# Issue order of stores, a skipped block and weight loads where an expert stage meets a feed-forward

## The chip, the cores and the metric

The kernel runs on one core of one Trainium2 chip. The metric is the device time of one execution in microseconds (us); the lower, the better. The core has a matrix engine (TensorE, PE in the profile, with its weight loads as PEld), a vector engine (VectorE, DVE), a scalar engine (ScalarE, ACT), GpSimd (POOL) and SyncE (SP), which here issues nearly all DMA transfers. Each engine works through its own instructions in the order of the program and waits on semaphores for the others. Transfers issued by SP stand in one queue.

## What is computed

Three layers in a row over 4608 tokens of width 512, all in float32: a decayed attention, a mixture of eight experts with one expert per token, and a feed-forward with squared ReLU.

```python
def _moe_ref(x, modality_id, w_gate, modality_bias, w1, w2):
    logits = x @ w_gate + modality_bias[modality_id]
    e_idx = np.argmax(logits, axis=1)
    ...
    for e in range(E):
        mask = e_idx == e
        h = np.maximum(x[mask] @ w1[e], 0.0)
        out[mask] = gate_w[mask, None] * (h @ w2[e])
    return out

def _moe2_ref(x, w_in, w_out):
    h = np.maximum(x @ w_in, 0.0)
    return h * h @ w_out
...
    x = attention output, (4608, 512)
    x = _moe_ref(x=x, **moe_kwargs)
    return _moe2_ref(x=x, **moe2_kwargs)
```

## The kernel before, in words

A float32 product is made of three products of halves: each operand is split into a high and a low part (names ending in h and l), and `three` and `six` issue the matmuls high x high, high x low, low x high (L787 to L789 in the expert stage, L1133 to L1135 in the feed-forward).

**The expert stage** (`phase12`) works on slots, groups of tokens of one expert. There are ten slots: "E" and 0 to 7 with 512 tokens each, and slot 8 (`NF`) with 256. Every slot has eight steps f = 0 to 7, so there are 80 steps, i = 0 to 79; step i = 71 is (`NF-1`, 7), and i = 72 to 79 are those of slot 8. In a step, `first` multiplies x by 128 columns of w1 and ScalarE and VectorE make hh and hl of the result (L803, L804), and `second` multiplies these by w2 into the banks y. TensorE is given `first` of step i+1 before `second` of step i. In slot 8 `first` and `second` are 12 matmuls each. The weights come as 80 blocks of 512 KB: `wload` (L400) loads one into a buffer wr, of which there are three, and `wsplit` splits it (L149 on ScalarE, L150 on VectorE) into a buffer wx (for w1) or wy (for w2) of the pool `wp`, which has ten. The function `wl` issues the loads up to three blocks ahead of the split. At f = 7 the finished slot is copied to ye and stored: yd<-ye (L834, "token sum" store, 1 MB, or 0.5 MB for slot 8) and sd<-ix (L835), which writes the token number of each place of the slot, 4 bytes each, to a table in device memory. GpSimd's later write of the next ix into the same buffer (L431) waits for that store.

**Work put among the last steps.** `combos` reads slot E's result back (eyr<-yd, L750), makes the seven products' operands x for the first feed-forward tile (t = 0) out of it, split into halves in the buffers x0 to x3, and stores each to xc (`put`, L762, 512 KB each) for later passes. `extras` writes out a block for tokens beyond the planned slots, which stands behind a branch (`tc.If`, L904); for these inputs it is skipped. It names its own buffers cwx, cwy, cwr and so on out of the same pools. On SP the far side of the skipped block has nine semaphore instructions, by which the engine takes up where its transfers stand, one for each lane of the queue and its own counter; the other engines wait there for their own counter alone. `wload2(m, j, pool)` loads weight block j of the feed-forward's matrix m (0 in, 1 out; w<-wc, L1012, two transfers of 896 KB each, halves); six calls make twelve transfers, into buffers of `cv` for (0, 0) and of `wp` for the others, which come free as the last steps finish.

**The feed-forward** (`phase3`) goes tile by tile, 9 tiles of 512 tokens in 3 passes. Its products are made with seven multiplications in place of eight. A unit of TensorE is `six` matmul groups issued as 6 matmuls per bank half; z (L1108, L1111) gathers the results and h (L1235, L1236) splits them for the second matrix. `Plan` takes all operations with model times and needs, and writes them out in the order of the model's start times; each engine then keeps that order. One stand-in operation of 8.0 us on the DMA queue opens the plan. `xprep(n)` prepares the next tile: it loads yr<-yd in two halves of 512 KB, copies and subtracts them into the buffers x (x<-yr, L1108 on ScalarE) and stores these to xc (L1124). A load of yr waits until the slots' yd have landed. Buffer x0 holds two operands, so a new x waits for the store of the old one to xc to be read out and for TensorE's last use.

Of the kernel before, what the change touches and what calls it, by code (L numbers as in the profile page):

```python
# [27 lines left out]
NF = 8  # L28
# [60 lines left out]
def kernel(ctx, tc, qT, kT, kN, vN, modT, w_gate, mbias, w1, w2, w_in, w_out,  # L89
# [574 lines left out]
    def phase12():  # L664
        with ExitStack() as c1:
# [79 lines left out]
            def combos():  # L745
                for _ in cs:
                    pass
                yr = cv.tile([P, KD, TS], F32, tag="w", name="eyr")
                tx = cv.tile([P, 2, 256], F32, tag="w", name="etx")
                sp.dma_start(yr, yd[:, 0:TS].rearrange("(c p) t -> p c t", p=P))  # L750
                yield 1
                xs = [cv.tile([P, 2, 2, 2, 256], F32R, tag="w", name=f"x{a}") for a in range(4)]
                b11, b12 = yr[:, 0:2, 0:256], yr[:, 0:2, 256:512]
                b21, b22 = yr[:, 2:4, 0:256], yr[:, 2:4, 256:512]

                def sub(o, a, b):
                    dve.tensor_tensor(out=o, in0=a, in1=b, op=ALU.subtract)

                def put(m, src):
                    t_ = held["x", m] = xs[m // 2][:, m % 2]  # L760
                    split(t_[:, 0], t_[:, 1], src, dve)
                    sp.dma_start(xc[0, m], t_.bitcast(F32).rearrange("p a k t -> p (a k t)"))  # L762

                sub(tx, b12, b11)
                put(0, b11)
                yield 1
                put(1, b21)
                yield 1
                sub(b12, b22, b12)
                put(2, b22)  # L770
                yield 1
                sub(b11, b22, tx)
                put(3, tx)
                yield 1
                put(5, b12)
                yield 1
                sub(b21, b21, b11)
                put(4, b11)
                yield 1
                put(6, b21)  # L780
                yield 1
# [28 lines left out]
            def second(u, cols=range(KD)):  # L810
# [9 lines left out]
                if f == 7:  # L820
# [5 lines left out]
                    if 3 not in cols:  # L826
                        return
                    ix = XG[s][1]
                    if s == "E":
                        yo, so = yd[:, 0:TS], sd[0:TS]  # L830
                    else:
# [6 lines left out]
            us = [(s, f) for s in seq for f in range(8)]  # L838
            wkeys = [(s, g) for s in seq for g in range(4)]
            nw = 2 * len(wkeys)  # L840
            st = {"ld": 4, "sp": 2}
            ex = combos()

            def wl(upto):
                while st["ld"] < min(upto, nw, st["sp"] + 3):
                    key = wkeys[st["ld"] // 2]
                    if key[0] not in ereg:
                        expert(key[0])
# [100 lines left out]
            for i, u in enumerate(us):  # L949
# [11 lines left out]
                    elif s != "E" and 3 <= f <= 6:  # L961
                        trans(nx, f - 3)
                if u == (NF, 7):
                    wload2(1, 0, wp)
                second(u)
                if s == "E" and f == 6:
                    trans(nx, 2)
# [18 lines left out]
                        pass  # L986
                    ws(8, 2, 11)
                else:
                    wl(i + 9)
                    fill(wsg(i + 6, 2 if i < 10 else 1, i + 9), part(cs, 2250))  # L990
                    if i >= 68:
                        run(ex, 3)
                    if i == 73:
                        assert next(cs, 0) == 0 and next(ex, 0) == 0
                        wload2(0, 0, cv)
                if u == (NF, 1):
                    wload2(0, 1, wp)
                if u == (NF, 4):
                    extras()
                if u == (NF, 5):  # L1000
                    wload2(0, 2, wp)
                if i == 6:
                    ext = nc.values_load(slots[0:1, 3, 0:1], min_val=0, max_val=NX)
            assert st["ld"] == st["sp"] == nw
# [77 lines left out]
    def phase3():  # L1082
        with ExitStack() as c2:
            ff = c2.enter_context(tc.tile_pool(name="ff", bufs=1))
            sb = lambda name, shape, dt=F32R: ff.tile(shape, dt, tag=name, name=name)
            plan = Plan()
            for j in (1, 2):
                wload2(1, j, wp, False)
            WT = [[[held["w", m, j, x] for x in range(2)] for j in range(3)] for m in range(2)]
            XT = [held["x", m] for m in range(7)]  # L1090
            HT = [sb(f"h{j}", [P, 2, 7, 256]) for j in range(3)]
# [204 lines left out]
            for n in range(9, len(T3)):  # L1296
                VO.append(VO[-1] if T3[n][1] == T3[n - 1][1] else 1 - VO[-1])
            plan.add([(DMA_, 8.0)], lambda e: None)
            loadw(0, 1, 1)
            for n, (p, t) in enumerate(T3):  # L1300
                nq = len(PASSES[p])
                order = sorted((7 * q + AT1[x], q, x) for q in range(nq) for x in AT1)
# [2 lines left out]
                if n + 1 < len(T3):  # L1305
                    if T3[n + 1][1] == t:
                        loadw(p + 1, 0)
                    xprep(n + 1)
                begin(n)
                for x in (1, 2, 5, 6, 7, 4, 3):  # L1310
# [45 lines left out]
```

## Time and profile before

| | us |
|---|---|
| median of 3 runs | 1433.48 |
| the runs | 1435.76, 1433.48, 1429.42 |
| profiled execution, as timed | 1429.32 |
| its span in the trace | 1427.6 |
| TensorE busy | 1359.1 (95% of the span) |
| VectorE, ScalarE, GpSimd busy | 1026.1, 632.1, 182.0 |
| feed-forward's first matmul | 657.7 into the span |

The three engines beside TensorE have room, so a change of the time shows where TensorE stands still or where its granted clock is low. The granted clock is given as a share of full speed: 1.00 is 2.4 GHz, 0.50 is 1.2 GHz. A wait is read together with what released it: an engine that waits for ScalarE may wait for a transfer that ScalarE waits for. In the rows "SPq" is SP's sequencer, "PEq" and "PEldq" that of TensorE.

### The profile page before, as it was taken

The page shows a single profiled execution, that of the slowest core. Times are in us where ns is not written, and L with a number is a line of the kernel's source. Part 1 is how long each engine was busy: PE and PEld are TensorE (multiplying, and loading weights), DVE is VectorE, ACT ScalarE, POOL GpSimd, SP SyncE. Part 2 cuts the span into 40 slices and gives each one's busy share as a digit, 9 for nine tenths or more (in the row PEclk, how much of TensorE's full clock was granted, in tenths as well). Part 3 has the DMA queues.
Part 4 walks back from the last instruction along what each step waited for, and adds up shares of the span by engine and source line. Part 5 has one row for each costly group of instructions (what it writes and reads, how often), then busy time and mean ns, then how long its engine had stood idle before and what let it go on. Part 6 is the DMA issues. An engine that isn't in the chain of part 4 may idle for free. (4 is left out here: it accounts for less than half of the span.)

```text
span 1427.6 us, 26428 instructions
## 1 busy us (share of the span) xinstructions
PE 1359.1 (95%) x10384; PEld 1250.9 (88%) x10384; DVE 1026.1 (72%) x2018; ACT 632.1 (44%) x1289; POOL 182.0 (13%) x164
## 2 busy tenths in 40 slices
PE   7999999999999999978899999999999999999994
PEld 6889877888788878868899999999999999999994
DVE  3777866877787788553788777777767777687674
ACT  1444444445445454342566555553334443343331
POOL 3222113101110010000212222100000000011122
PEclk9999999999999999998999999999999999999998
DMA  9977247988899897898544455587445564677672
GB/s 341 378 269 275 90 165 237 260 254 213 317 279 262 234 324 198 236 270 265 190 163 171 184 197 213 208 312 267 163 177 204 214 218 163 271 275 266 237 253 101
DMA packets 143733, 332.40 MB, mean 233 GB/s; under 512 B 20208, under 2 KB 54512, under 8 KB 143600
## 3 DMA queue, kind: packets, MB, share of 16 engines
q1 hardware_dynamic: 135520, 310.06, 65.0%
q0 software_dynamic: 5920, 19.40, 3.6%
q8 instruction: 83, 1.36, 0.4%
q10 hardware_dynamic: 2160, 1.17, 0.3%
q14 instruction: 50, 0.41, 0.1%
HBM read 222.57 MB, written 108.02 MB: 232 GB/s over the span
## 5 line engine op out<-in xcount | busy, mean ns | idle before, releaser
L1133 PE MATMUL bank<-w,h 128*128 128x256 f32 x1008 | 285.5, 283 | 16.1 <-ACT h L1235 5.8
L1134 PE MATMUL bank<-x,w 128*128 128x256 f32 x1008 | 285.9, 284 | 4.2 <-DVE x L1111 4.1
L1133 PE MATMUL bank<-x,w 128*128 128x256 f32 x1008 | 286.0, 284 | 2.3 <-DMA x<-xc 1.4
L1135 PE MATMUL bank<-w,h 128*128 128x256 f32 x1008 | 284.2, 282 | 1.2 <-DVE h L1236 1.1
L1135 PE MATMUL bank<-x,w 128*128 128x256 f32 x1008 | 285.3, 283 | 0.0
L1134 PE MATMUL bank<-w,h 128*128 128x256 f32 x1008 | 284.1, 282 | 0.0
L1108 ACT ACTIVATE z<-bank 128x256 f32<-128x256 f32 x288 | 110.4, 383 | 274.0 <-PE bank L1135 272.5
L1133 PEld LDWEIGHTS bank<-w,h 128*128 128x128 f32 x1008 | 191.6, 190 | 19.2 <-ACT h L1235 7.4
L1134 PEld LDWEIGHTS bank<-x,w 128*128 128x128 f32 x1008 | 193.5, 192 | 5.4 <-DVE x L1111 5.4
L1133 PEld LDWEIGHTS bank<-x,w 128*128 128x128 f32 x1008 | 193.1, 192 | 2.9 <-DMA x<-xc 1.6
L1135 PEld LDWEIGHTS bank<-x,w 128*128 128x128 f32 x1008 | 193.4, 192 | 0.0
L1135 PEld LDWEIGHTS bank<-w,h 128*128 128x128 f32 x1008 | 191.2, 190 | 2.2 <-DVE h L1236 2.2
L1235 ACT ACTIVATE h<-z 128x512 fp32r<-128x512 f32 (+2 forms) x270 | 156.9, 599 | 81.5 <-DVE z L1111 70.6
L1134 PEld LDWEIGHTS bank<-w,h 128*128 128x128 f32 x1008 | 191.3, 190 | 0.3 <-DMA w<-wc 0.2
L1236 DVE TENSOR_TENSOR h<-z,h 128x512 fp32r<-128x512 f32 (+2 forms) x270 | 173.3, 661 | 12.1 <-ACT h L1235 11.7
L1111 DVE TENSOR_TENSOR z<-z,bank 128x256 f32<-128x256 f32 x216 | 90.2, 418 | 63.1 <-PE bank L1135 42.3
L787 PE MATMUL bank<-hh,wy 128*128 128x512 f32 (+1 forms) x320 | 126.9, 397 | 5.7 <-ACT hh L803 5.7
L787 PE MATMUL bank<-xh,wx 128*128 128x512 f32 (+1 forms) x320 | 124.6, 389 | 3.9 <-PEq L904 3.9
L788 PE MATMUL bank<-xl,wx 128*128 128x512 f32 (+1 forms) x320 | 124.5, 389 | 1.1 <-DVE xl L743 1.1
L788 PE MATMUL bank<-hl,wy 128*128 128x512 f32 (+1 forms) x320 | 124.4, 389 | 1.0 <-DVE hl L804 1.0
L789 PE MATMUL bank<-xh,wx 128*128 128x512 f32 (+1 forms) x320 | 124.0, 388 | 0.0
L789 PE MATMUL bank<-hh,wy 128*128 128x512 f32 (+1 forms) x320 | 123.7, 387 | 0.0
(168 smaller groups left out, 2212.9 us busy)
## 6 DMA issues: line engine op xcount, KB each, us to landing
x<-xc SPq DMA_DIRECT2D x112, 512.0 KB
wr<-w SPq DMA_DIRECT2D x80, 512.0 KB
xc<-x SPq DMA_DIRECT2D x63, 512.0 KB
w<-wc SPq DMA_DIRECT2D x32, 896.0 KB
wc<-cwh SPq DMA_DIRECT2D x16, 896.0 KB
wc<-cwl SPq DMA_DIRECT2D x16, 896.0 KB
pd<-oe SPq DMA_DIRECT2D x24, 512.0 KB
xd<-xs SPq DMA_DIRECT2D x9, 1024.0 KB
```

The lines of the kernel that those rows point to most:

```text
L787: pe.matmul(ps, lh, rh, start=first, stop=False)
L788: pe.matmul(ps, lh, rl, start=False, stop=False)
L789: pe.matmul(ps, ll, rh, start=False, stop=last)
L1108: plan.add(a_(c), lambda e: e.activation(o, i, f), r, w)
L1111: plan.add(engs or d_(c), lambda e: e.tensor_tensor(out=o, in0=a, in1=b, op=op), r, w)
L1133: e.matmul(ps[n], lh, rh, start=first and n == 0, stop=False, skip_group_check=True)
L1134: e.matmul(ps[n], lh, rl, start=False, stop=False, skip_group_check=True)
L1135: e.matmul(ps[n], ll, rh, start=False, stop=True, skip_group_check=True)
L1235: plan.add(a_(c), lambda e: e.activation(h[:, 0, a:b], z[:, a + 1:b + 1], AF.Copy), rs, ks[0])
L1236: plan.add(d_(c), lambda e: e.tensor_tensor(out=h[:, 1, a:b], in0=z[:, a + 1:b + 1], in1=h[:, 0, a:b].bitcast(F32), op=ALU.subtract), rs + ...
```

## The change

Five things are done, all of them to the order in which work is issued.

1. The seven stores of the first tile's x to xc leave `combos` (L762). They are operations of the feed-forward's plan now, ahead of the preparation of the second tile.
2. `extras`, the skipped block, moves from the end of step (`NF`, 4) to the end of step (`NF-1`, 7), i = 71. All its lines count one higher in the changed file (L905 for L904).
3. At i = 70 and 71 the loads of expert weights go one block ahead of the split in place of three, and at i = 72 none is issued.
4. The feed-forward's weight loads are issued at other steps: (0, 1) at (`NF`, 2) for (`NF`, 1), (0, 2) at (`NF`, 4) for (`NF`, 5), (1, 0) at (`NF`, 5) for (`NF`, 7), (1, 1) at (`NF`, 7), and (1, 2) in the last `second`, ahead of the store of yd. The last two stood in the plan before.
5. The plan has no weight loads for its first pass any more; its stand-in of 8.0 us stays.

```diff
@@ combos / put
                     split(t_[:, 0], t_[:, 1], src, dve)
-                    sp.dma_start(xc[0, m], t_.bitcast(F32).rearrange("p a k t -> p (a k t)"))
@@ second
                     ix = XG[s][1]
+                    if s == NF:
+                        wload2(1, 2, wp)
@@ phase12
-            st = {"ld": 4, "sp": 2}
+            st = {"ld": 4, "sp": 2, "few": False}
...
-                while st["ld"] < min(upto, nw, st["sp"] + 3):
+                while st["ld"] < min(upto, nw, st["sp"] + (1 if st["few"] else 3)):
...
                 if u == (NF, 7):
-                    wload2(1, 0, wp)
+                    wload2(1, 1, wp)
                 second(u)
...
-                    wl(i + 9)
+                    st["few"] = i in (70, 71)
+                    if i != 72:
+                        wl(i + 9)
...
-                if u == (NF, 1):
+                if u == (NF, 2):
                     wload2(0, 1, wp)
+                if u == (NF - 1, 7):
+                    extras()
                 if u == (NF, 4):
-                    extras()
+                    wload2(0, 2, wp)
                 if u == (NF, 5):
-                    wload2(0, 2, wp)
+                    wload2(1, 0, wp)
@@ phase3
-            for j in (1, 2):
-                wload2(1, j, wp, False)
...
-            loadw(0, 1, 1)
...
+                    if n == 0:
+                        for m in range(7):
+                            dma(xc[0, m], XT[m].bitcast(F32).rearrange("p a k t -> p (a k t)"), 512,
+                                [("x", m, 0), ("x", m, 1)], [("xc", 0, m)])
                     xprep(n + 1)
```

What SP's queue holds shows the order. The first place is slot 7's stores and the skipped block, on SP before (wr are expert weights, w000 to w011 feed-forward weights):

```order
L834 DMA yd_93<-ye_5857 128x4x512
L835 REGISTER_ALU
L835 DMA sd_94<-ix_5146 128x4x1
L400 ISA
L400 DMA wr2_5876<-w2 128x2x512
L1012 DMA w000_5940<-wc_95 128x1792
L1012 DMA w001_5942<-wc_95 128x1792
L1012 DMA w010_5944<-wc_95 128x1792
L1012 DMA w011_5946<-wc_95 128x1792
L904 COMPARE_AND_BRANCH
```

The same place on SP after, up to the branch:

```order
L750 DMA eyr_5723<-yd_93 128x4x512
L400 ISA
L400 DMA wr2_5770<-w2 128x2x512
...
L835 DMA yd_93<-ye_5848 128x4x512
L836 REGISTER_ALU
L836 DMA sd_94<-ix_5146 128x4x1
L905 COMPARE_AND_BRANCH
```

And on SP after, from the far side of the skipped block to the first loads of yr:

```order
L400 DMA wr1_8934<-w1 128x4x256
L400 ISA
L400 DMA wr2_8936<-w2 128x2x512
L1017 DMA w000_8969<-wc_95 128x1792
...
L1017 DMA w121_9151<-wc_95 128x1792
...
L836 DMA sd_94<-ix_5525 128x2x1
L1127 DMA xc_97<-x0_5726 128x1024
L1127 DMA yr_9179<-yd_93 128x2x512
L1127 DMA xc_97<-x0_5726 128x1024
L1127 DMA yr_9179<-yd_93 128x2x512
```

Two loads of expert weights moved behind the block, the block directly behind sd of slot 7, and all twelve loads w000 to w121 ahead of the last yd and sd.

The second place is the start of the feed-forward on SP before, from the far side of the block:

```order
L1012 DMA w101_9124<-wc_95 128x1792
L832 TENSOR_LOAD slots_100
L832 ISA x2
L834 REGISTER_ALU
L834 DMA yd_93<-ye_9138 128x4x256
L835 REGISTER_ALU
L835 DMA sd_94<-ix_5525 128x2x1
L1124 DMA w110_9163<-wc_95 128x1792
...
L1124 DMA yr_9173<-yd_93 128x2x512 x2
```

There four weight loads stood between sd and yr; now two stores xc stand among the loads of yr, and the weights are ahead.

The third place is ScalarE in the first tile of the feed-forward, before (z gathers results, h splits them, x<-yr prepares the second tile):

```order
L1108 ACTIVATE z1_9171<-bank6_90 128x256
L1108 ACTIVATE z2_9172<-bank5_89 128x256
L1108 ACTIVATE z1_9171<-bank6_90 128x256
L1108 ACTIVATE z1_9171<-z1_9171 128x256
L1108 ACTIVATE z2_9172<-bank5_89 128x256
L1235 ACTIVATE h1_9168<-z1_9171 128x768
L1235 ACTIVATE h0_9167<-z0_9170 128x512
L1108 ACTIVATE z2_9172<-bank5_89 128x256
L1108 ACTIVATE x0_5726<-yr_9173 128x512
L1235 ACTIVATE h2_9169<-z2_9172 128x512
```

And ScalarE after, at the same place:

```order
L1111 ACTIVATE z1_9177<-bank6_90 128x256
L1111 ACTIVATE z2_9178<-bank5_89 128x256
L1111 ACTIVATE x0_5726<-yr_9179 128x512 x2
L1111 ACTIVATE z1_9177<-bank6_90 128x256
L1111 ACTIVATE z2_9178<-bank5_89 128x256
L1111 ACTIVATE z1_9177<-z1_9177 128x256
L1238 ACTIVATE h1_9174<-z1_9177 128x768
```

The two x<-yr copies moved up, from behind the third copy of z2 to directly behind the first, ahead of a copy of z1 and one of z2.

The matmuls of TensorE keep their order there up to the second half of the first tile (unit numbers count from 0; these are the first matmuls of units 14 to 18 after; each waits for the copy that frees its bank):

```order
L1136 MATMUL bank6_90<-x3_5729,w010_9004 128x256
...
L1136 MATMUL bank5_89<-x2_5728,w020_9064 128x256
...
L1136 MATMUL bank4_88<-x1_5727,w010_9004 128x256
...
L1136 MATMUL bank7_91<-x1_5727,w020_9064 128x256
...
L1136 MATMUL bank5_89<-x2_5728,w020_9064 128x256
```

Units 15 and 18 both write bank5, so the second waits until z2 of the first has been copied.

## Rows read from the trace of the kernel before

**Rows 1.** The page's busy times of each engine, over the whole span.

```profile
PE 1359.1 (95%) x10384; PEld 1250.9 (88%) x10384; DVE 1026.1 (72%) x2018; ACT 632.1 (44%) x1289; POOL 182.0 (13%) x164
```

**Rows 2.** Waits, 600 to 720 us, TensorE's: us in total, times, longest.

```profile
PE bank L1133 <- ACT h L1235: 5.8, 1, 5.8
PE bank L787 <- ACT hh L803: 5.7, 1, 5.7
PE bank L787 <- PEq L904: 3.9, 1, 3.9
```

**Rows 3.** Stretches: us, busy PE, PEld, DVE, ACT, POOL, PEclk, DMA share, GB/s.

```profile
634.40:640.10 5.70, 0.04 (x1) 0.04 (x1) 0.33 (x1) 1.42 (x3) 0.00 (x0) 0.69 0.93 208
640.10:644.00 3.90, 3.16 (x12) 2.67 (x12) 1.56 (x3) 0.18 (x1) 0.00 (x0) 0.50 1.02 418
...
648.00:653.00 5.00, 5.00 (x24) 5.00 (x24) 0.42 (x1) 0.39 (x1) 0.00 (x0) 0.50 0.64 234
...
657.70:676.80 19.10, 19.05 (x158) 18.67 (x156) 10.79 (x24) 7.51 (x18) 0.00 (x0) 1.00 0.94 226
661.00:670.00 9.00, 9.00 (x77) 9.00 (x76) 5.69 (x13) 4.90 (x13) 0.00 (x0) 1.00 0.91 51
670.00:681.00 11.00, 6.75 (x55) 6.37 (x53) 4.26 (x9) 1.42 (x3) 0.00 (x0) 1.00 0.95 388
676.80:682.60 5.80, 0.08 (x1) 0.09 (x1) 0.10 (x1) 1.28 (x3) 0.71 (x1) 0.86 0.65 255
```

**Rows 4.** Timeline of ScalarE, 608 to 683: start, us, what, [idle before, releaser].

```profile
610.18 1.15 ACT L149 ACTIVATE x<-eyr 128x512 fp32r<-128x512 f32 x2 [7.46 <-DMA eyr<-yd]
...
638.68 1.06 ACT L149 ACTIVATE wy<-wr 128x1024 fp32r<-128x1024 f32 x1 [9.55 <-DMA wr<-w]
...
667.23 0.39 ACT L1108 ACTIVATE z<-bank 128x256 f32<-128x256 f32 x1 [0.17 <-PE bank L1135]
...
681.32 0.63 ACT L1108 ACTIVATE x<-yr 128x512 fp32r<-128x512 f32 x1 [9.38 <-DMA yr<-yd]
```

**Rows 5.** Timeline of SP, 600 to 672: the transfers it issues.

```profile
604.42 0.51 SPq L750 DMA_DIRECT2D eyr<-yd  x1
...
624.49 0.39 SPq L835 DMA_DIRECT2D sd<-ix  x1
625.15 0.71 SPq L400 DMA_DIRECT2D wr<-w  x1
...
658.28 0.40 SPq L834 DMA_DIRECT2D yd<-ye  x1
...
659.56 2.98 SPq L1124 DMA_DIRECT2D w<-wc  x4
667.61 2.59 SPq L1124 DMA_DIRECT2D yr<-yd  x2
```

**Rows 6.** Timelines of SP and GpSimd: sd of two earlier slots.

```profile
483.13 0.39 SPq L835 DMA_DIRECT2D sd<-ix  x1
...
493.53 0.22 POOL L431 COPY ix<-tab 128x4 int32 x1 [27.15 <-DMA sd<-ix]
...
530.16 0.41 SPq L835 DMA_DIRECT2D sd<-ix  x1
...
544.24 0.29 POOL L431 COPY ix<-tab 128x2 int32 x1 [28.47 <-DMA sd<-ix]
```

**Rows 7.** Line L904, the skipped block: count, ns each, first and last start.

```profile
L904 SPq EVENT_SEMAPHORE  x9: 17/17/17, 639.3 to 648.5; - x9
L904 POOLq EVENT_SEMAPHORE  x6: 17/30/43, 558.1 to 560.1; - x6
L904 POOLq COMPARE_BRANCH  x1: 50/50/50, 555.8 to 555.8; - x1
...
L904 SPq COMPARE_BRANCH  x1: 53/53/53, 629.4 to 629.4; - x1
...
L904 PEldq COMPARE_BRANCH  x1: 6312/6312/6312, 641.5 to 641.5; - x1
```

## The prediction

> **What bounds the kernel now.** I first read the page's busy times: TensorE works 95% of the span [rows 1], so the time can change only where TensorE stands still or runs at the lower clock, and the stretch the edit touches is 600 to 700 us of the trace. The waits of that stretch name three stops of TensorE that belong together [rows 2]: 5.7 us for hidden values from ScalarE (L803), 3.9 us on its own sequencer at the skipped block (L904), 5.8 us for h from ScalarE (L1235) in the feed-forward. The stretch table puts them at 634.4 to 640.1, at about 644 to 648, and at 676.8 to 682.5, and shows the granted clock at 0.50 (the lower level, 1.2 GHz) after the first: 24 matmuls in 5.0 us, 0.208 each, against 158 in 19.05 us, 0.1206 each, at 1.00 [rows 3].
>
> Then I asked what stood behind each wait of ScalarE. Before 640 its split of the last weight block (wy) had waited 9.55 us for a load [rows 4] that SP issued at 625.15, directly behind the token-sum store yd and the index store sd (624.49) [rows 5]. Before 682.5 its copy x<-yr had waited 9.38 us [rows 4] for the loads of yr issued at 667.61; ahead of them in the queue lie yd, sd of the last slot (658.28 and the next issue) and four weight loads [rows 5]. In both places the queue is slow behind sd: from 661 to 670 it moves 51 GB/s, then 388 [rows 3]. This is no single event: sd of two earlier slots was issued at 483.13 and 530.16, and GpSimd's next write of ix, which waits for it, began at 493.53 and 544.24, 10.4 and 14.1 us later [rows 6]; the other slots lie between. A store of 2 KB therefore costs the queue as much as 4 MB of loads.
>
> **Stage A, up to the feed-forward.** The edit takes seven stores xc (0.5 MB each) out of SP's queue before yd/sd, and puts the skipped block directly behind sd of slot 7. What the skipped block does on SP: it leads past nine semaphore instructions [rows 7], which in the changed order wait for the last transfer of each lane of the queue; the lanes of yd and sd are among them. So SP leaves the block when sd has landed: 624.49 + 10.4 to 14.1 = 634.9 to 638.6, and I take the middle, 636.7. The weight loads of steps 78 and 79, one of which before was issued at 625.15 and the other earlier still, now follow the block. Issue costs 0.7 (624.49 to 625.15 [rows 5]). Landing: eyr, 1 MB, was used 5.76 us after its issue (604.42, 610.18 [rows 4, 5]); the half-size load less 0.5 MB at about 0.4 MB/us, 4.5, and 5.8 as upper end. 636.7 + 0.7 + 4.5 = 641.9 for ScalarE's split, 1.06 [rows 4], then hh at about 0.4 and a hand-over: TensorE, which by ScalarE's order has run dry after step 76's first half (about 633), goes on at R = 643.5 to 643.8, bounds 641.7 to 646.5. Eight halves of 12 matmuls are left, 96: about 25 at the lower clock as before (25 x 0.21 = 5.3), 71 at 0.1175 (8.35, an estimate from the 0.1206 above less idle records). The stage ends at 657.3 (655.3 to 660.2) against 657.7 before. The stop at L803 of 5.7 and the one at the block of 3.9 vanish, and one stop of 10 to 11 us takes their place: **net 0, -2 to +2.5.**
>
> The block itself moves on every engine. On TensorE it now comes while 512-wide matmuls run. The row of GpSimd, whose branch came amid ordinary traffic, lasts about 2.3 us (555.8 to the first semaphore at 558.1), TensorE's 6.3 at 641.5, amid the weight loads [rows 7]. The sequencer runs ahead by the 12 matmuls that were still executed after it branched (640.1 to 644 [rows 3]), some 2.5 us. So 2.3 is hidden, 6.3 leaves 3.8; I take 0.5, and any of it is swallowed by the wait until R, since TensorE stops there anyway.
>
> TensorE's branch at the block lasts 6312 ns [rows 7] and costs it 3.9 us [rows 2]. The Trainium skill, page "Advanced Engine Details and Errata", section "Control Flow Timing", gives about 108 ns for a compare-and-branch, with which this trace does not agree. By that figure alone the block would be passed in 0.1 us on each engine, SP would issue the next load at about 625.3, TensorE would resume near 640 and the sum below would be about +8 instead of +9.6, inside the forecast's own range.
>
> **Stage B, the start of the feed-forward.** All twelve weight loads (0.917 MB each) now stand in the queue ahead of yd and sd of the last slot, where before four stood behind them. With the two expert loads that is 12.06 MB from 637.4 on. At 0.41 MB/us (between 0.388 and 0.418 [rows 3]) this takes 29.4 us, with 1.5 for the start and for buffers that come free late: 668.3. TensorE needs yd's landing next: 0.5 MB, 1.3, 669.6. Then the slow 9 us behind sd, 678.6. Then xc0, yr#1, xc1, yr#2, 2.1 MB at 0.39, 5.4, and 0.6 as before between the end of such a sum and the use (670 + 4.2 MB/0.39 = 680.7, used at 681.32 [rows 3, 4]): 684.6, against 681.32 for the first half of yr before.
>
> What decides is where those copies stand on ScalarE. Before, x<-yr followed the z2 copy that frees TensorE's bank for unit 21, and TensorE went on to unit 26 (158 matmuls recorded in that stretch, 26 units of 6 [rows 3]). Now both x<-yr copies stand ahead of the z1 and z2 copies that follow the unit-12 copy of z2; unit 18 waits for the z2 copy of unit 15. TensorE stops after 18 units, at 657.3 + 18 x 0.72 = 670.3, until both copies (0.63 each [rows 4]; the second from 684.6) and two copies of 0.4 are through: 686.3. Before it resumed at 682.5 after 26 units. The lag is (686.3 - 682.5) + 8 units x 0.72 = 3.8 + 5.8 = **9.6 us**. The lower clock after the stop is as before. Low end: sd early (-1.8) and the slow time half as long (-4.5), since nothing shows how much of it belongs to the store and how much to what is queued: +3.3. High end: sd late (+1.9), landing 5.8 (+1.3), rate 0.388 (+1.7): +14.5.
>
> What follows is bound by TensorE, so the lag stays. The seven xc stores now run beside the second tile: 3.7 MB in a tile's time of over 20 us, behind yr, so at nothing; were the queue full there, the copies for the next tile would come up to 9 us late, against a whole tile of lead. Fewer DMAs at 611 to 622 give nothing: TensorE does not wait there [rows 2].
>
> **The sum.** 1429.3 (the profiled execution, as timed) + 0 + 9.6 = 1438.9. That execution is 4.2 us under the median of the three, 1433.5; against the median the sum is 1443.1.
>
> **Rivals.**
> Same: the slow time behind the last sd is short, because the queue is less deep behind it (four weight loads fewer). For it: that slot has 256 tokens, so its store is half as large. Against: 51 GB/s for 9 us was seen behind that very store [rows 3]. Result +3.3, 1432.6 here, 1436.8 against the median, within 0.5%, 7.2 us, which is about what a measurement can tell from no change.
>
> Faster: the nine waits are already met when SP comes, so the expert loads leave at 625 and the slow time is not the store's but came from the traffic around it (the seven xc writes before, now gone). Then the stops of 5.7 and 3.9 and the excess of 38 slow matmuls (38 x 0.09 = 3.4) go, 13 us, the stage ends near 645. That alone gains little: with a slow 9 us left, the second yr would be used at about 673 and TensorE resume at 675, lag -7.5 + 5.8 = -1.7. It decides only if the slow time behind the last sd is under some 3 us as well; then -11, 1418, 1422 against the median. Against it: the two sd rows of slots without any xc store [rows 6].
>
> Worse: SP's code for the far side of the block is fetched through the same slow queue. For it: SP's branch at 629.4 saw its first semaphore only at 639.3, 9.9 us later, and the last at 648.5 [rows 7]. If a second fetch falls after sd has landed, 4 us are added to R and to everything behind it: +13.6 to +15, 1447 to 1449 against the median. It counts as slower.
>
> **Chances.** The forecast (slower by 7 to 13) 0.45, worse 0.13, together 0.58 for slower by over 0.5%; same 0.30; faster by over 0.5% 0.12. The likeliest is the forecast: 1443. The forecast's own range is 1440 to 1447. The range to hold 8 in 10 takes in the same case down to -3.5, 1430, and the worse one to +17.5, 1451; below lie about 0.12, above 0.07.
>
> **What would show it.** In the changed kernel: SP's semaphore rows at L905 ending 10 to 14 us after sd of slot 7, at 635 to 639; one stop of TensorE of 9 to 12 us from about 633 for hh from ScalarE, and none at L905; the stage's end at 655 to 660; ScalarE waiting for yr from about 668 to 684, 15 us; a stop of TensorE of about 16 us after 18 units; 8 to 9 us at under 80 GB/s behind the last sd. Wrong would be: a wx load that lands before 635, a slow time under 4 us, or TensorE passing unit 18 before yr has landed.

## The result and the profile of the changed kernel

The changed kernel takes 1443.76 us (median of 6 runs, 1442.66 to 1449.85), the kernel before 1434.13 (6 runs, 1429.42 to 1436.9). The ratio is 1.0069 with a 95% interval of 1.0048 to 1.009: slower by 0.7%, 9.6 us between the medians. Forecast were a slower kernel, a lag of 9.6 us, and 1443 (1443.1 by its sum).

The profiled execution of the changed kernel took 1449.85, its slowest run, and that of before 1429.32, its fastest. So the traces are compared by stretches. The issue of sd of slot 7 stands at 624.49 before [rows 5] and at 631.87 after; these 7.4 us arose in the first 250 us, where the edit touches nothing (the first yd is issued at 248.52 and at 256.52).

| stretch | before, us | after, us | difference |
|---|---|---|---|
| up to the issue of sd of slot 7 | 624.49 | 631.87 | +7.4 |
| from there to the first matmul of the feed-forward (657.67, 664.44) | 33.18 | 32.57 | -0.6 |
| from there to the third pass, a wait of 0.47 us of TensorE for z at 1225.01 and 1242.76 | 567.34 | 578.32 | +11.0 |
| from there to the end of the span | 202.6 | 205.3 | +2.8 |

The last row is not the edit's either: TensorE's stops after 1200 us add up to 10.8 us before and 13.5 after, and to between 10 and 16 us in the traces of the experiments, in no order with the edits. By these two traces the edit did -0.6 + 11.0 = 10.4 us, beside the 9.6 of the medians and the 9.6 of the forecast.

The page of the changed kernel, busy times, answers to [rows 1]:

```profile
PE 1361.6 (94%) x10384; PEld 1254.7 (87%) x10384; DVE 1024.2 (71%) x2018; ACT 632.2 (44%) x1289; POOL 180.5 (12%) x164
```

TensorE has the same work in a longer span; the time went into its stops.

The waits of the changed kernel from 600 to 720 us answer to [rows 2] (us in total, times, longest):

```profile
PE bank L1136 <- ACT z L1111: 18.7, 1, 18.7
PE bank L786 <- DVEq L905: 7.6, 1, 7.6
...
PE bank L787 <- DVE hl L803: 0.9, 1, 0.9
PE bank L786 <- ACT hh L802: 0.8, 1, 0.8
```

The three stops of before have become two. One of 18.7 us at z in the feed-forward has replaced that of 5.8 at h, and one of 7.6 behind VectorE's sequencer at the block (DVEq L905) has replaced those of 5.7 and 3.9.

The stretch table of the changed kernel, with the columns of [rows 3], shows where TensorE stands and what the queue moves meanwhile:

```profile
629.90:637.50 7.60, 0.04 (x1) 0.00 (x0) 1.38 (x2) 2.25 (x4) 0.00 (x0) 0.81 0.47 144
649.50:664.40 14.90, 13.21 (x96) 13.02 (x97) 4.40 (x7) 4.00 (x10) 0.00 (x0) 0.89 0.99 399
664.40:677.50 13.10, 13.10 (x110) 12.94 (x108) 7.13 (x17) 4.84 (x12) 0.00 (x0) 1.00 1.01 414
677.50:696.20 18.70, 0.04 (x1) 0.00 (x0) 0.67 (x2) 1.79 (x5) 2.37 (x2) 0.63 0.71 177
...
680.00:690.00 10.00, 0.00 (x0) 0.00 (x0) 0.00 (x0) 0.00 (x0) 0.00 (x0) 0.62 0.39 36
```

In the third row TensorE runs 13.1 us into the feed-forward, which is 18 units of 0.72 (110 matmul records), and in the fourth it stands still. The last row is the slow time behind the last sd, 36 GB/s, with no engine at work.

The timeline of SP in the changed kernel, 631 to 690, answers to [rows 5] (start, length, what is issued):

```profile
631.23 0.40 SPq L835 DMA_DIRECT2D yd<-ye  x1
631.87 2.12 SPq L836 DMA_DIRECT2D sd<-ix  x1
645.36 1.17 SPq L400 DMA_DIRECT2D wr<-w  x2
646.59 18.37 SPq L1017 DMA_DIRECT2D w<-wc  x12
665.78 0.40 SPq L835 DMA_DIRECT2D yd<-ye  x1
...
688.21 0.39 SPq L1127 DMA_DIRECT2D yr<-yd  x1
...
689.17 0.42 SPq L1127 DMA_DIRECT2D yr<-yd  x1
```

And that of ScalarE, to [rows 4]:

```profile
648.87 1.06 ACT L149 ACTIVATE wx<-wr 128x1024 fp32r<-128x1024 f32 x1 [4.58 <-DMA wr<-w]
...
692.46 0.63 ACT L1111 ACTIVATE x<-yr 128x512 fp32r<-128x512 f32 x1 [18.08 <-DMA yr<-yd]
695.04 0.63 ACT L1111 ACTIVATE x<-yr 128x512 fp32r<-128x512 f32 x1 [1.95 <-DMA yr<-yd]
```

The last yd was issued at 665.78, behind twelve weight loads; yr could be issued only when it had landed, at 688.21, and was used at 692.46 and 695.04. SP's own waits in that stretch name the landing of yd:

```profile
SPq L1127 <- DMA yd<-ye: 15.1, 1, 15.1
```

TensorE went on at 696.26, 31.8 us into the feed-forward; before it went on at 682.52, 24.9 us into it, and had eight units more behind it.

The lines at the block in the changed kernel answer to [rows 7]:

```profile
L905 SPq EVENT_SEMAPHORE  x9: 17/17/17, 641.4 to 644.3; - x9
...
L905 PEldq EVENT_SEMAPHORE  x1: 51/51/51, 630.5 to 630.5; - x1
L905 DVEq COMPARE_BRANCH  x1: 72/72/72, 632.2 to 632.2; - x1
...
L905 DVEq EVENT_SEMAPHORE  x1: 21/21/21, 637.5 to 637.5; - x1
```

SP leaves the block at 644.3, 12.4 us after it issued sd. TensorE's own sequencer is past the block at 630.5, 0.6 us after the end of its last matmul at 629.9. VectorE comes to its branch at 632.2 and is past it at 637.5, and in the same instant, 637.55, TensorE goes on. So 2.3 of the 7.6 us of TensorE's stop lie before VectorE's branch (its split of wx, ahead of the branch, had waited 2.13 us for ScalarE's), and 5.3 between the branch and the far side.

### The profile page after: what moved, and what is told of

It reads as the page before. It is cut to its first block, busy times and chain, and to the rows that moved or that the text cites. A ratio compares the mean times of both kernels' runs of the same rounds, so it can differ in the third digit from the quotient of the medians.

```text
span 1448.1 us, 26435 instructions
## 1 busy us (share of the span) xinstructions
PE 1361.6 (94%) x10384; PEld 1254.7 (87%) x10384; DVE 1024.2 (71%) x2018; ACT 632.2 (44%) x1289; POOL 180.5 (12%) x164
## 5 line engine op out<-in xcount | busy, mean ns | idle before, releaser
L1136 PE MATMUL bank<-w,h 128*128 128x256 f32 x1008 | 285.1, 283 | 13.1 <-DVE oe L1114 7.8
L1239 DVE TENSOR_TENSOR h<-z,h 128x512 fp32r<-128x512 f32 (+2 forms) x270 | 172.0, 658 | 22.9 <-ACT h L1238 22.4
```

The lines of the kernel that those rows point to most:

```text
L1136: e.matmul(ps[n], lh, rh, start=first and n == 0, stop=False, skip_group_check=True)
L1239: plan.add(d_(c), lambda e: e.tensor_tensor(out=h[:, 1, a:b], in0=z[:, a + 1:b + 1], in1=h[:, 0, a:b].bitcast(F32), op=ALU.subtract), rs + ...
```

## The experiments

Three things were to be told apart: what part of the loss is the place of the copies on ScalarE, what part the order on the queue, and what the skipped block and the store sd cost by themselves. Each run's ratio is to the kernel before, run beside it on the same chip; since the median of before lay between 1435 and 1439 there, the ratios are compared, not the microseconds. The stretch "A" goes from the issue of slot 7's yd to the first matmul of the feed-forward, "B" from there to a wait of 0.69 us of TensorE for oe in the second tile, which every trace has (722.37 before, 740.08 after). Each kernel has one trace. Up to the feed-forward the changed kernel, e1 and e2 have the same order but for e2's last four weight loads, and their A is 33.2, 36.3 and 35.1: a difference of 3 us in A is no more than that spread.

| kernel | ratio (95% interval) | A, us | B, us |
|---|---|---|---|
| before | 1 | 33.8 | 64.7 |
| changed | 1.0069 (1.0048 to 1.0090) | 33.2 | 75.6 |
| e1 changed, copies late | 0.9932 (0.9910 to 0.9955) | 36.3 | 56.4 |
| e2 changed, two weight blocks behind | 1.0048 (1.0024 to 1.0073) | 35.1 | 72.5 |
| e3 before, stores xc late | 0.9980 (0.9960 to 1.0000) | 32.8 | 67.1 |
| e4 before, block early | 0.9993 (0.9974 to 1.0012) | 32.7 | 66.5 |
| e5 changed, sd on the other queue | 0.9989 (0.9973 to 1.0005) | 30.0 | 66.0 |
| e6 before, copies late | 0.9984 (0.9965 to 1.0004) | 34.8 | 62.3 |
| e7 before, both | 0.9926 (0.9898 to 0.9953) | 27.6 | 57.7 |
| e8 changed, both | 0.9945 (0.9923 to 0.9967) | 29.8 | 57.3 |
| e9 as e7, block in mid-slot | 0.9920 (0.9893 to 0.9947) | 21.4 | 57.6 |
| e10 as e7, block at a slot's end | 0.9969 (0.9947 to 0.9991) | 21.2 | 58.1 |
| e11 changed, no block | 1.0019 (1.0004 to 1.0035) | 30.2 | 72.9 |
| e12 before, no block | 0.9977 (0.9961 to 0.9994) | 27.5 | 66.1 |

In e9 and e10 the block's price lies ahead of A, since the block stands in an earlier slot.

### e1: the copies later on ScalarE

```diff
-            plan.add([(DMA_, 8.0)], lambda e: None)
+            first_ready = [("b", i, j) for i in range(2) for j in range(2)]
+            first_ready += [("xc", 0, m) for m in range(7)]
+            plan.add([(DMA_, 22.0)], lambda e: None, (), first_ready)
```

The stand-in operation had no operation depending on it, and the plan put it behind the loads of yr, whatever its length: with 16, 20, 24 or 28 us in its place the order of the first tile came out the same. Here the loads of yr and the stores xc depend on it.

> The changed kernel with one edit: the plan is told that xc and yr start 22 us into the feed-forward, so that ScalarE's two x<-yr copies stand some 20 rows later; the order on the queue up to the first four loads of yr and their neighbours stays. Theory (the loss is the place of the copies on ScalarE, in front of work that TensorE waits for): TensorE passes unit 18 without a stop, the 18.7 us stop becomes one of under 3 us, and the time falls by 14 to 18 us, to 1426 to 1430. Rival (the loss is the lateness of yr itself, whatever the order, because the second tile needs it): a stop of 10 us or more stands elsewhere and the time stays at 1440 or above.

Measured: 0.9932, which against the changed kernel's 1.0069 is 1.4%, 19 to 20 us; the two traces differ in B by 19.2 us, while A, with nothing changed in it, came out 3.1 longer. Waits of e1, 600 to 720 us:

```profile
PE bank L786 <- DVEq L905: 7.4, 1, 7.4
...
PE bank L786 <- ACT hh L802: 3.4, 1, 3.4
...
ACT x L1111 <- DMA yr<-yd: 2.9, 2, 1.5
PE bank L1136 <- ACT oe L1111: 1.4, 2, 0.7
```

The stop of 18.7 us is gone, and nothing took its place: yr came hardly earlier (issued at 690.01 and 690.97, 22 and 23 us into the feed-forward, in the changed kernel 24 and 25), but ScalarE waits for it 2.9 us in all and TensorE not at all. The rival falls. So the whole of the loss, and more, hangs on the order of the first tile's operations. The edit moved more than the two copies, though: the plan also put TensorE's first matmuls of the second tile, which in the changed kernel stand after 210 matmul records of the feed-forward, behind all 252 of the first tile. In the old order, without the stop, TensorE would have come to them about 27 us in (an estimate: 46.4 in the changed kernel's trace less the 19.5 by which the stop shifted them), and e1's two copies began 26.3 and 28.9 us in. With the copies alone moved, a wait of a few us for x may have been left; no run shows it. The gain is larger than expected because the stop of 5.8 us that the kernel before has in B is gone too.

### e2: two weight blocks behind the last yd and sd again

```diff
-                    if s == NF:
-                        wload2(1, 2, wp)
...
+                second(u)
                 if u == (NF, 7):
                     wload2(1, 1, wp)
-                second(u)
+                    wload2(1, 2, wp)
```

> The changed kernel with the feed-forward's weight blocks (1, 1) and (1, 2), 3.7 MB, behind the last yd and sd again, as before the change. Theory (yd has to queue behind the backlog of weights): yd lands about 8 us earlier after its issue, but yr then queues behind these 3.7 MB; x<-yr begins 2 to 5 us earlier than in the changed kernel, and the time is 1439 to 1442. Rival (the backlog does not matter, only the slow time behind sd): no difference, 1443 to 1445.

Measured: 1.0048; the intervals of e2 and of the changed kernel overlap, so the difference of 3 us between the ratios is inside what the runs can tell. In the traces B is 3.1 us shorter and A 1.9 longer. Waits of e2:

```profile
PE bank L1135 <- ACT z L1110: 15.7, 1, 15.7
PE bank L786 <- DVEq L903: 11.8, 1, 11.8
```

yr was issued 13.7 us after the last yd in place of 22.4, as expected, but its first use came 25.0 us into the feed-forward in place of 28.0, and 1.9 of these 3.0 us are the feed-forward's own later start: the stop at the block happened to be 4 us longer. That leaves 1.1 us for the backlog ahead of yd, if it is a part of the loss at all: what the queue does not carry ahead of yd, it carries ahead of yr.

### e3 and e4: one part of the change alone, in the kernel before

```diff
@@ e3: the stores xc go into the plan
-                    sp.dma_start(xc[0, m], t_.bitcast(F32).rearrange("p a k t -> p (a k t)"))
...
+                    if n == 0:
+                        for m in range(7):
+                            dma(xc[0, m], XT[m].bitcast(F32).rearrange("p a k t -> p (a k t)"), 512,
+                                [("x", m, 0), ("x", m, 1)], [("xc", 0, m)])
@@ e4: the block goes to the end of step 71
-                if u == (NF, 4):
+                if u == (NF - 1, 7):
                     extras()
```

e4 also holds the loads of expert weights back as the change does.

> The kernel before with one part of the change: the seven stores xc of the first tile go into the plan. The plan then puts x<-yr about five copies later on ScalarE than before, and the stores no longer stand ahead of yd and sd of slot 7. Theory: the expert stage keeps its stops of 5.7 and 3.9 (the load behind sd stays where it was, so the stores ahead did not make it slow), the stop of 5.8 at h goes since the copies stand later, and yr comes about 2.5 us later: 1426 to 1431. Rival (the seven stores ahead of sd made the queue slow): the stop of 5.7 at hh shrinks under 2.

> The kernel before with one part of the change: the skipped block moved to the end of step 71, with the loads of expert weights held back as in the change; the stores xc and the feed-forward's other loads stay as before. Theory: the stops of 5.7 and 3.9 go and one stop of 9 to 12 us for the weight load behind the block takes their place, so the start of the feed-forward moves by under 2.5 us and the time is within 1432 to 1437. Rival (the move of the block is the loss, not the start of the feed-forward): 1440 or above.

Measured: 0.9980 and 0.9993, intervals up to 1.0000 and 1.0012. Neither part is the loss by itself. Waits of e3, then of e4:

```profile
PE bank L786 <- PEq L903: 4.3, 1, 4.3
PE bank L786 <- ACT hh L802: 3.4, 1, 3.4
...
PE bank L1133 <- DMA w<-wc: 2.3, 1, 2.3
PE bank L1132 <- DMA w<-wc: 1.9, 1, 1.9
```

```profile
PE bank L787 <- DVEq L904: 10.3, 1, 10.3
PE bank L1135 <- ACT h L1237: 5.7, 1, 5.7
```

In e3 the stop at h is gone because the plan put x<-yr later, and two short stops for weight loads that stand behind sd came up instead: 2.9 us gained between the medians' ratios where 3 to 8 were expected, and in the trace A and B together are 1.4 us longer than before, so this stretch does not show the gain. The stop for hh fell from 5.7 to 3.4, between the two theories. In e4 the stops of 5.7 and 3.9 became one of 10.3, and A stayed within 1.2 us. The size was forecast, the name was not: it is VectorE's passage past the block and not the weight load that TensorE waits for.

### e5: the index store on GpSimd's queue

```diff
-                    sp.dma_start(so.rearrange("(j p) -> p j", p=P), ix[:, :wd // P])
+                    pool.dma_start(so.rearrange("(j p) -> p j", p=P), ix[:, :wd // P])
```

GpSimd also reads the slot's place into a register of its own.

> The changed kernel with one edit: the index stores sd of all slots are issued by GpSimd, on its own queue, instead of SP. Theory (the slow time is the store of 4-byte elements itself, and it holds up only the queue that it is in): SP leaves the skipped block some 3 to 5 us after yd's issue instead of 13, the weight loads behind the block come before ScalarE wants them, TensorE's stop at the block remains only as far as VectorE's code fetch takes (2 to 4 us); yr is issued 8 us sooner behind yd and the stop at unit 18 falls from 18.7 to 8 to 11. Together 10 to 16 us under the changed kernel, a ratio to the kernel before of 0.995 to 1.000. Rival (the small elements occupy the 16 DMA engines, whatever queue they come from): stops and ratio as in the changed kernel, 1.005 to 1.009.

Measured: 0.9989, 0.8% under the changed kernel. Waits of e5, then the issues of SP at the start of the feed-forward:

```profile
PE bank L1137 <- ACT z L1112: 8.4, 1, 8.4
PE bank L786 <- DVEq L906: 7.2, 1, 7.2
```

```profile
663.88 0.39 SPq L836 DMA_DIRECT2D yd<-ye  x1
...
675.46 0.39 SPq L1128 DMA_DIRECT2D yr<-yd  x1
```

yr goes out 11.6 us after the last yd, not 22.4. But GpSimd does not wait for yd: it issued the last two index stores at 566.61 and 578.50, long before SP's yd of slots 7 and 8 (632.14 and 663.88). Its store at 578.50, SP's next two transfers, and the rows of three stretches (columns as in [rows 3]):

```profile
578.50 0.74 POOL L837 DMA_DIRECT2D sd<-ix  x1 [11.08 <-issue]
```

```profile
579.70 0.50 SPq L726 DMA_DIRECT2D wc<-cwh  x1
580.42 0.34 SPq L726 DMA_DIRECT2D wc<-cwl  x1
```

```profile
580.80:590.00 9.20, 9.20 (x41) 7.40 (x40) 5.25 (x8) 6.22 (x9) 0.00 (x0) 1.00 0.38 32
590.00:594.00 4.00, 4.00 (x19) 3.23 (x18) 3.74 (x5) 2.08 (x3) 0.00 (x0) 1.00 1.05 432
664.00:675.00 11.00, 11.00 (x94) 11.00 (x93) 6.83 (x16) 3.85 (x9) 0.00 (x0) 1.00 0.97 380
```

With no sd near, the queue moves 380 GB/s behind the last yd: the slow time belongs to the store and went away with it. The edit did not show, however, that it holds up only the queue that it is in. Behind the sd of 578.50, SP's two stores of 896 KB crawl at 32 GB/s for 9.2 us, although sd stands in GpSimd's queue, and then the rate is 432. Behind the sd of 476.06 it is 32 GB/s from 481.4 to 490.0, with three loads of 512 KB issued by SP between 480.0 and 481.4. That speaks for the rival's mechanism, elements that slow all queues; its forecast of the time failed because the stores now fall where loads are not urgent. So the gain comes from when the stores are issued. Whether the 4-byte size is the reason was not tried, as no run stores the same 2 KB in larger pieces.

SP is past the block 7.1 us after yd's issue (639.2; 3 to 5 were expected), and the load of step 78 is no longer waited for. The stop behind VectorE stayed at 7.2, though: it was expected to shrink to 2 to 4. With no sd near, it does not hang on it.

### e6 to e8: late copies and the other queue, in both kernels

e6 makes the stand-in of 8 us effective in the kernel before, as e1's diff does with 22 in the changed one; e7 adds e5's edit to that; e8 is the changed kernel with both and 18 us. In e7 to e10, as in e5, GpSimd issues the last two sd early (at 570.42 and 582.85 in e7).

> The kernel before with one edit: its plan's stand-in of 8 us on the DMA queue is made to precede the loads of yr, so that ScalarE's x<-yr copies stand about 10 rows later. Nothing else differs. Theory (the place of the copies decides, in this kernel as in the changed one): the stop of 5.8 us at h before 682.5 goes, with about 2 us of lower clock after it: 6 to 8 us, a ratio of 0.994 to 0.996, and level with or a little under the changed kernel with late copies (0.9932). Rival (yr is needed just as early elsewhere): ratio 0.998 to 1.002.

> The kernel before with late copies (as in the run on that alone) and the index stores sd on GpSimd's queue. Theory: the load behind sd of slot 7 lands 8 us sooner, so the stop of 5.7 at hh goes, TensorE comes to the block at full clock and the gap there stays at 2 to 4: 6 to 10 us under late copies alone, a ratio of 0.987 to 0.990. Rival (sd's elements slow every queue): level with late copies alone.

> The changed kernel with late copies (the plan's start at 18 us here, since yr comes sooner) and sd on GpSimd's queue. Theory: both stops shrink; against late copies in the changed kernel alone (0.9932) another 4 to 7 us, from the stop at the block, a ratio of 0.988 to 0.991. Rival: 0.993.

Measured: 0.9984 (its interval takes in 1), 0.9926, 0.9945. Waits of e6, then of e7:

```profile
PE bank L787 <- ACT hh L803: 6.7, 1, 6.7
PE bank L787 <- PEq L904: 3.5, 1, 3.5
PE bank L1134 <- DMA w<-wc: 2.9, 2, 1.8
```

```profile
PE bank L787 <- PEq L905: 2.4, 1, 2.4
...
PE bank L787 <- ACT hh L803: 1.1, 1, 1.1
```

e6 gained 2.3 us where 6 to 8 were expected. The stop at h went, but with the copies out of the way TensorE ran into the next late thing, the four weight loads behind sd (2.9, and 0.7 in another group). In e1 these loads stand ahead of sd, there is no such stop, and late copies gave 19 us; the intervals of e1 and e6 do not meet. That points to the change's early weight loads as a gain that the copies hid. It is argued from the stops: no run moved these loads alone. With sd out of that stretch (e7) these stops go as well, the stop for hh falls from 6.7 to 1.1, and 10 to 11 us are gained, though less than the 14 to 19 expected. e8 does not gain on e1, where 4 to 7 us were expected: its stop behind VectorE is still 7.3, and though A and B together are 5.6 us shorter in its trace, its interval overlaps those of e1 and e7.

### e9 and e10: the block elsewhere

e9 is e7 with `extras()` at the end of step (6, 2), e10 with it at the end of (6, 7), where steps are 512 wide; the expert loads are held back around it as in the change.

> The kernel before with late copies and sd on GpSimd's queue, and the skipped block moved to the end of step (6, 2), in the middle of a slot of 512-wide steps, with the expert loads held back around it. Theory (at the block TensorE stands still because VectorE, in order, needs about 5 us to get past it, and hh/hl of the next steps come late; a step of 24 matmuls of 0.234 takes 5.6 us, so most of that is hidden in a wide step, unlike in the 256-wide ones of the changed kernel): a stop of 0 to 3 us at the block, and the stop of 2.4 us on TensorE's sequencer in the last slot goes; 0 to 4 us under the same kernel with the block at its old place (0.9926), a ratio of 0.990 to 0.993. Rival (a skipped block costs TensorE its own fetch wherever it stands): a stop of 3.5 to 7 us at the block, a ratio of 0.993 to 0.997.

> As the run with the block in the middle of a slot, but at the end of step (6, 7), the same place of a slot as in the changed kernel (behind the finished slot's stores), where the next steps are 512 wide. Theory: VectorE's 5 us behind the block are hidden as in the middle of a slot, 0 to 3 us of stop, a ratio of 0.990 to 0.993; if SP's wait for the landing of yd delays the expert loads (about 6 us), ScalarE waits for one of them and the stop is 3 to 5. Rival (place in the slot decides, not the width): a stop of 7 us as in the changed kernel, 0.995 or above.

Measured: 0.9920 and 0.9969. Waits of e9, then its rows of VectorE and of TensorE's sequencer at the block:

```profile
PE bank L787 <- DVEq L905: 5.3, 1, 5.3
```

```profile
L905 DVEq COMPARE_BRANCH  x1: 72/72/72, 559.2 to 559.2; - x1
L905 PEldq EVENT_SEMAPHORE  x1: 51/51/51, 560.7 to 560.7; - x1
...
L905 DVEq EVENT_SEMAPHORE  x1: 21/21/21, 562.6 to 562.6; - x1
```

My theory falls here: wide steps hid neither stop. It is 5.3 us in the middle of a slot and 11.7 at a slot's end (e10), where the rival of e10 (0.995 or above) held; both end with VectorE. In e9 TensorE's own sequencer is past the block only at 560.7, 3.3 us into the stop, so that much would have stood without VectorE, and e9's rival, a stop of 3.5 to 7 us from TensorE's own passage, is not excluded by e9 alone. In e10 TensorE had waited 4.4 us when VectorE came to its branch at 591.1, and the passage then took 7.1; GpSimd had issued an sd at 582.24 and the rate was 72 and 62 GB/s from 588 to 592, which may be the reason, but was not tested. e9's ratio lies in the range that the theory gave, but for another reason: what the block costs there, it saves in the last slot, where A is 6.2 us shorter than in e7. Why TensorE waits for VectorE at all is in the order of the changed kernel: TensorE's first matmul behind the block writes a bank that the block names as well, and waits for VectorE's counter, which VectorE raises on the far side of the block. So TensorE cannot run ahead of VectorE there, however much work it has.

### e11 and e12: no block

The surplus block is left out; for these inputs it does nothing.

> The changed kernel without the surplus block (left out; these inputs have no surplus tokens). The order of everything else stays. Theory (two things bind in turn at the end of the expert stage: VectorE's way past the block, and the weight load behind sd): the stop of 7.6 us for VectorE goes, the load for step 78 goes out directly behind sd but lands only 12 to 14 us later, so TensorE stops 4 to 7 us for hh; the stage ends 2 to 5 us earlier, yr comes 2 to 5 us earlier, the stop at unit 18 stays at 16 to 19. Ratio to the kernel before 1.002 to 1.006. Rival (the block alone is the loss of the expert stage): no stop above 2 us there, ratio under 1.000.

> The kernel before without the surplus block (left out, as in the run beside). Theory: the stop of 3.9 at TensorE's sequencer goes, the stop of 5.7 at hh and that of 5.8 at h stay: 3 to 5 us, ratio 0.9965 to 0.998. Rival (the gap is covered by something else that comes out, a weight load): ratio 0.999 to 1.001.

Measured: 1.0019, 0.0001 under the range of the theory, and 0.9977, inside it. In e12 the stop at TensorE's sequencer is gone as expected; those at hh and h are 4.0 and 4.5, and one of 1.5 for a weight load came up. Waits of e11:

```profile
PE bank L1134 <- ACT z L1109: 15.4, 1, 15.4
ACT wx L149 <- DMA wr<-w: 9.9, 1, 9.9
...
PE bank L786 <- ACT hh L802: 6.1, 1, 6.1
```

Without the block, TensorE in the changed kernel stops 6.1 us for hh, because of the load behind sd. This is the stop that the prediction named. With the block it is covered by the 7.6 us for VectorE. The two bind in turn, which is why A differs by only 3 us, and B by another 2.7. The ratios put the block's price in the changed kernel at 0.5%, 7 us, and their intervals do not meet.

## Why the prediction was right, point by point

**Stage A, net 0 (-2 to +2.5).** Measured -0.6. The chain of the load is right nearly term by term, once 7.4 us are taken off the changed kernel's times: SP left the block 12.4 us after sd's issue (12.2 was taken), ScalarE's split of wx began at 641.5 (641.9 forecast), the stage ended at 657.1 (657.3 forecast). What failed is the step on the block. It asked about TensorE's own branch and priced it at 0.5 us; this was right (its branch at 626.7 was through at 630.5, 0.6 us after the last matmul), but the same step left out that VectorE passes the block too, in 5.3 us, and that TensorE needs VectorE past it. The stop of 7.6 us therefore came 10 us sooner than the one named, and when TensorE reached the point where it had been expected to run dry, it waited 0.8 and 0.9 us and not 10. The forecast of "none at L905" was wrong. The time was right because the load ended the stage either way: e11 shows it, 6.1 us for hh when the block is away. That this stop stayed hidden under the same load was luck, as the forecast did not know of it.

**The rule on branches.** The Trainium skill, page "Advanced Engine Details and Errata", section "Control Flow Timing", has about 108 ns for a compare-and-branch. The instruction row itself is short on VectorE (72 ns), but from it to the next instruction on the far side of the block 5.3 us pass in the changed kernel and 3.4 in e9, and TensorE stood 5.3 to 11.8 us in the runs where the block came early. The measurement decides; the estimate that the prediction gave by that page's figure, +8, for which it shows no sum, would have been too low by about 2. It also let SP go on at once, where SP left the block 12.4 us after it issued sd.

**Stage B, +9.6.** Measured +11.0. The mechanism is the one named: TensorE stopped after 18 units, at the z2 copy behind two x<-yr copies. e1 shows that the order of the first tile is the loss: with it changed, B is 19.2 us shorter. The term that was mis-sized is the arrival of yr. 29.0 us from the start of the feed-forward to TensorE's going on were forecast, 31.8 measured. The forecast let yd land at 669.6, ahead of the slow time, and had the loads of yr under way when that ended, at 678.6. But yd landed only at the end of the slow time: SP waited 15.1 us for it and issued yr at 688.21, which is 680.8 with 7.4 taken off. That is 2.2 us late. From there to the use of the second half of yr 6.8 us passed (6.0 were taken), and to TensorE another 1.2 (1.7 taken). A part of the 2.2 is the backlog: the rate was still 317 GB/s from 678 to 679 and 134 in the next us, where 669.6 + 7.4 = 677.0 had been taken for its end.

The 9.6 of the forecast holds 0.4 us by which stage A was to end sooner (657.3 against 657.7), so stage B by itself was 10.0, and 1.0 more was measured. The later yr made 2.8. One us came back because TensorE ran at the lower clock (0.50) for 3.1 us after its stop (696.26 to about 699.4) where it had run so for 5.1 before (682.52 to about 687.6); the forecast had put these equal. The other 0.8 is not located. That forecast and medians agree to 0.1 us is therefore luck; the runs of each kernel spread over 7 us.

**The slow time behind sd.** The prediction left open how much of it belongs to the store. e5 answers: nearly all, as it went away from behind the last yd with the store and came up behind the store's new place. It is also what makes the rival "same" fail: the queue behind was less deep, and the slow time was as long.

**The rival "faster"** named two conditions and needed both. Neither was met: SP left the block only at 644.3, 12.4 us after it issued sd, and the slow time was 10 us. The rival "worse" wanted 4 us more before TensorE goes on with hh. That came at 650.25, which is 642.9 with 7.4 taken off, where 643.5 to 643.8 had been forecast, so it did not occur either.

**What the prediction did not ask:** whether TensorE needs yr so early at all. In e6 it went on to the second tile in the order of the kernel before and waited for weights, not for yr; in e1 it did so with the second tile's first matmuls moved back as well.

The fastest kernels measured are e9 (0.9920), e7 (0.9926) and e1 (0.9932), which the runs cannot tell apart. They are 0.7% to 0.8% under the kernel before and 1.4% to 1.5% under the changed one.

## What to carry to other kernels

When a change makes transfers come later, look first at what stands behind their consumer on its in-order engine: a copy that waits 18 us costs TensorE all of it if the next copy frees a bank, and in e1, where it stood some twenty rows later, it cost nothing. A delay that a planner is told of counts only if operations depend on it; check in the order that it moved something. A block that is skipped at run time is to be costed on every engine, and by what the engines wait for across it, not by the branch. When a store is moved to another engine's queue, look at when that engine issues it before the queue is given the credit.

## What the runs showed of the hardware

- Behind the store of the last slot's 256 elements of 4 bytes the queue moved 51 and 36 GB/s for 9 and 10 us. With the stores issued by GpSimd (0.8 us each) the slow time came behind their new places and slowed SP's transfers there: 32 GB/s for 9.2 us behind the one of 578.50 (e5).
- From its branch at a skipped block to the far side VectorE took 3.4 to 9.6 us (e9, and 632.1 to 641.7 in e2). The 9.6 fell into the slow time behind sd, but so did 5.3 (changed) and 5.1 (e1). TensorE's own branch row lasted 3.4 to 6.8 us; it was the last to hold TensorE up, for 2.4 to 4.3 us, only in kernels with the block in the last slot (before, e3, e6, e7).
- The first 250 us of the program, equal in both kernels, differed by 8.0 us between the two profiled executions, among it a stop of TensorE of 5.4 us at 246.47 of the changed kernel, where that of before had stops of 1.2 and 1.7. The spread of each kernel's runs, 0.5%, is of this size.
